# Order of the dense units as a list, half weight tiles, banks for each half of the first chunk, and the last adds on GpSimd

## The chip, the core and the metric

The kernel runs on one core of one Trainium2 chip. Its engines are TensorE (PE; PEld is its weight load), VectorE (DVE), ScalarE (ACT), GpSimd (POOL) and SyncE (SP, which here only issues transfers). Each engine executes its own instructions in the order in which they stand in the program and waits for the others by semaphores. The metric is the device time of one execution in microseconds (us); less is better. The time before is 863.67 us, the median of 3 runs (863.49 to 864.08).

## What is computed

The input is 2048 tokens of 512 features. A layer norm feeds two branches: windowed attention with 32 heads of 16 features, in which each token sees itself and the 255 before it, and a SwiGLU feed-forward with 1792 hidden features. The second branch gates the first.

```python
xn = layernorm(x)                                  # 2048 x 512
q, k, v = split_heads(xn @ wqkv)                   # 32 heads of 16
scores = where(0 <= i - j < 256, q @ k.T * 16**-0.5, -1e9)
s = (softmax(scores) @ v) @ wo
f = (silu(xn @ w_gate) * (xn @ w_up)) @ w_down
out = x + s * silu(f)
```

All is fp32. Each operand of a dense matmul is split in a high part (the value rounded to the type fp32r) and a low part (what is left), and three products, high with high, high with low and low with high, are added up.

## The kernel before

The kernel is a program that writes out a schedule. While it is built, it keeps a clock of its own for each engine, and hands out instructions in the order in which that clock says they can run; the chip then runs this fixed order.

The 2048 tokens are four chunks of 512. The dense work is cut in 120 units, each with one weight tile of up to 128 x 1024 values. `Proj` (A) makes q and k of two groups of four heads, `Values` (V) makes v of half the heads, `GateUp` (G) makes one block of 128 hidden features, `Down` (D) adds a quarter of the hidden features to half of the output columns, `Wo` (W) is the attention's output product for half of the columns. A name like G1.7 is chunk 1, block 7. `dense_order` sets the order of the units from due times of A and V and a fixed row of G, D and W. A unit has two items, one bank of PSUM each, and PE's array is used as two halves of 64 rows: each half does its 64 features of an item, then the halves change items. A small DVE copy (`handover`, tile `ho`) stands between the two.

Between the dense matmuls PE runs the attention of 32 groups of heads: `b` are scores for the row maximum (DVE adds the mask and takes the maximum, tile `jk`), `c` are scores again, of which ACT makes the exponentials `p` and POOL masks the edges, and `pv` is the product with v. q and k go through DRAM (`qkd`) to be laid out anew, and so do the outputs of the attention (`od`, and the sums' reciprocals `den`, `rd`, read back as `o` and `r`).

For each unit, SP fetches its weights into a raw tile (`wr`, by `w_fetch`), ACT copies the high part (`wh`, L413) and POOL subtracts to get the low part (`wl`, L418), in pieces of 512 columns. There are three pairs of tiles of 1024 columns, so unit j can be split when unit j - 3 has ended (`w_split`, `item_end`), and unit j + 2 is fetched when unit j is split.

At the start (the head), the four token tiles of chunk 0 are loaded, normalised on ACT or DVE (`xt`, with the root `rs` made on POOL), and turned on PE into four banks `xp`, one for each 128 features, with all 512 tokens in one bank (`x_turn`). ACT then copies the high part `xh` (L332) and DVE subtracts the low part `xl` (L320), for tokens 0 to 255 and 256 to 511 apart. Dense matmuls begin when all four tiles are turned. The first unit is A0.0. Until then PE runs matmuls on a tile of ones (`warm`).

At the end (the tail), W3.0 and W3.1 are the last units, the last with four items of 128 tokens. `finish` multiplies an item by the gate (L813), adds x (L820) and stores it; in the last chunk all of this is on DVE, in the others the sum is on POOL.

Of the kernel before, what the change touches and what calls it, by code (L numbers as in the profile page):

```python
# [10 lines left out]
F32R = mybir.dt.float32r  # L11
# [6 lines left out]
P = 128  # L18
# [22 lines left out]
SPARE = 3  # L41
MW = 80
# [12 lines left out]
def tile_window_attention_swiglu_gate(  # L55
# [138 lines left out]
    def constants2():  # L194
# [117 lines left out]
    turned = []  # L312

    def x_split(k, part, pb, t, free):
        n = slice(256 * part, 256 * part + 256)
        hi, lo = (xn[0][s][:, k, n] for s in range(2))

        def low(t):
            xhigh[k, part] = t
            do("V", t, 0.42, lambda: nc.vector.tensor_tensor(lo, pb[:, n], f32(hi), op=ALU.subtract), done, -0.5)  # L320

        def done(t):
            xlow[k, part] = t
            if part == 0:
                return
            free(t)
            xready[0, k] = t
            if k == KC - 1:
                for i in range(4):
                    give(xt.pop((0, i)))  # L330

        do("S", t, 0.33, lambda: nc.scalar.activation(hi, pb[:, n], AF.Copy), low, -2.0)  # L332
# [3 lines left out]
    def x_turn(i):  # L336
        if not turned:
            turned.extend((bank(p, f"xp0_{k}"), p) for k, p in enumerate((rb_free, rb_free, fb_free, fb_free)))
        for k in range(KC):
            nc.tensor.matmul(  # L340
                turned[k][0][0][:, i * P : (i + 1) * P], xt[0, i][:, k * P : (k + 1) * P], ident,
                is_transpose=True, start=True, stop=True,
            )
        advance(0.45)
        seen.add(i)
        part = i // 2
        if {2 * part, 2 * part + 1} <= seen:
            for k in range(KC):
                (pb, tag), p = turned[k]
# [11 lines left out]
    class Unit:  # L361
# [3 lines left out]
        def wts(self, r):  # L365
            return wtile[self.n]


# [6 lines left out]
    ended_unit = {}  # L375

    def w_fetch(j):
# [16 lines left out]
        dma(now[0], go, then, slack=1.0, kb=512 if j > 2 else 400)  # L394

    raw = {}
    wpart = {}

    def w_split(j):
        if j not in landed or (j >= 3 and j - 3 not in ended_unit):  # L400
            return
        t = max(landed.pop(j), ended_unit.get(j - 3, 0.0))
        w = weighted[j].width
        hi, lo = [], []
        cuts = [(a, min(a + 512, w)) for a in range(0, w, 512)]
        left = [len(cuts)]

        def high(a, b):
            if not hi:
                hi.append(sb(f"wh{j}", [P, 1024], F32R, "wh", 3))  # L410
                lo.append(sb(f"wl{j}", [P, 1024], F32R, "wl", 3))
                wtile[j] = [hi[0], lo[0]]
            nc.scalar.activation(hi[0][:, a:b], raw[j][:, a:b], AF.Copy)  # L413

        def low(a, b):
            if j == 0 and a == 0:
                nc.gpsimd.tensor_copy(spare, xt[0, list(normed)[-1][1]][:, :1])
            nc.gpsimd.tensor_tensor(lo[0][:, a:b], raw[j][:, a:b], f32(hi[0][:, a:b]), op=ALU.subtract)  # L418

        def done(t, a):  # L420
            wpart[j, a, 1] = t
            left[0] -= 1
            if left[0] == 0:
                wready[j] = t
                if j:
                    timer(t - 0.5, w_fetch, j + 2)

        def after_high(t, a, b, sl):
            wpart[j, a, 0] = t
            do("G", t, 0.17 + 0.0021 * (b - a), lambda: low(a, b), lambda t: done(t, a), sl, lambda: len(normed) >= 4)  # L430

        for n, (a, b) in enumerate(cuts):
            sl = (0.0 if j >= 3 else 0.2) + 0.3 * n
            if j == 0:
                sl = -3.0 + 0.1 * n
            do("S", t, 0.13 + 0.00078 * (b - a), lambda a=a, b=b: high(a, b),
               lambda t, a=a, b=b, sl=sl: after_high(t, a, b, sl), sl)
# [3 lines left out]
    def item_end(j, t):  # L441
        item_ended[j] = item_ended.get(j, 0) + 1
        if item_ended[j] == 2 * weighted[j].items:
            ended_unit[j] = t
            w_split(j + 3)
# [8 lines left out]

    def xt_ready(c, k):
        return latest([*(normed.get((c, t)) for t in range(4)), bank_time(rb_free, 2)])
# [36 lines left out]
    PAIRS = ((0, 0), (0, 1), (1, 0))  # L493

    class Stationary(Unit):
# [3 lines left out]

# [7 lines left out]
        def mms(self, i, r, pb):  # L507
            w = [t.rearrange("p (a k n) -> p a k n", a=2, k=KC) for t in self.wts(r)]
            xs = xn[self.c % 2]
            if self.c == 0 and self.n == 0 and i == r:  # L510
                for a, b in ((0, 0), (1, 0), (0, 1)):
                    for part in range(2):
                        n = slice(256 * part, 256 * part + 256)
                        for k in range(KC):
                            def go(first, last, k=k, a=a, b=b, n=n):
                                return mm(pb[:, n], w[a][half(r), i, k, :], xs[b][half(r), k, n], first, last)
                            yield 256, go, lambda k=k, a=a, b=b, part=part: latest(
                                [(xlow if b else xhigh).get((k, part)), wpart.get((0, 512 * i, a))]
                            )
# [958 lines left out]
```

## Time and profile before

| what | value |
| --- | --- |
| median of 3 runs | 863.67 us |
| the profiled execution, its time | 865.33 us |
| its span, first to last instruction | 863.6 us |
| granted TensorE clock, mean | 0.998 |
| PE busy | 854.2 us (99%), 11960 matmuls |
| PEld, POOL, ACT, DVE busy | 785.1, 595.9, 495.7, 486.2 us |
| DMA | 139.58 MB, mean 162 GB/s |

The profile is of one execution. A row of a timeline gives the start and the length in us, the engine, the line, the work with its tiles as out<-in, and how many instructions it covers; in brackets stands the idle time of the engine just ahead of it and what ended that. A row of PE's waits gives who was waited for, then the total in us, how many waits, and the longest. The chain of waits follows the last instruction back to what released it. Tiles' numbers are left out in these rows.

### The profile page before, as it was taken

To read this page: it belongs to the slowest core of one execution; us is meant where nothing else is said; L and a number is where in the kernel's file an instruction comes from. 1 tells how busy PE (TensorE), PEld (TensorE's weight loads), DVE (VectorE), ACT (ScalarE), POOL (GpSimd) and SP (SyncE) were. 2 spreads that over 40 slices of the span, in tenths; PEclk is the share of its full clock that TensorE was granted. 3 is DMA by queue.
4 is the path that set the end of the run, shared out by engine and by line. 5 is a ranking of instruction groups with operands and counts; after the bars stand their busy time and mean duration, and the time that the engine had idled before them with its cause. 6 is when DMAs were issued, how large, how long until landed. Compare 5 with 4: busy or idle time off the path is not lost.

```text
span 863.6 us, 29615 instructions
## 1 busy us (share of the span) xinstructions
PE 854.2 (99%) x11960; PEld 785.1 (91%) x11960; DVE 486.2 (56%) x1633; ACT 495.7 (57%) x1056; POOL 595.9 (69%) x630
## 2 busy tenths in 40 slices
PE   9999999999999999999999999999999999999997
PEld 8999999899799898999799999999999989889897
DVE  4364566555566555656565656566556656645234
ACT  4355555546665566565677566655656665656532
POOL 7555566658776775666879586666668697869764
PEclk9999999999999999999999999999999999999999
DMA  5764645455756963464777866455556668553241
GB/s 176 198 179 132 195 112 172 142 156 153 195 154 183 275 171 111 96 181 123 174 201 185 223 183 192 108 174 136 165 135 174 176 188 223 166 147 113 87 149 62
DMA packets 67628, 139.58 MB, mean 162 GB/s; under 512 B 12690, under 2 KB 21394, under 8 KB 67492
## 3 DMA queue, kind: packets, MB, share of 16 engines
q1 hardware_dynamic: 67204, 137.17, 57.3%
q8 instruction: 94, 1.54, 0.8%
q10 hardware_dynamic: 288, 0.52, 0.2%
q14 instruction: 42, 0.34, 0.2%
HBM read 107.74 MB, written 29.62 MB: 159 GB/s over the span
## 4 chain that ended last, share of the span: by engine, by line
PE 94%; DMA 3%; DVE 1%; ACT 1%; issue 0%; SPq 0%; POOL 0%; DVEq 0%; POOLq 0%; ACTq 0%
PE u L451 18%; PE d L451 18%; PE g L451 18%; PE a L451 11%; PE pv L1152 8%; PE c L1115 5%; PE s L451 5%; PE vp L451 5%; PE b L961 5%; DMA r<-rd 1%; DMA wr<-wgu 1%; DVE jk L969 0%; DMA xt<-x 0%; PE xp L469 0%; ACT wh L413 0%
## 5 line engine op out<-in xcount | busy, mean ns | idle before, releaser
L418 POOL TENSOR_TENSOR wl<-wr,wh 128x512 fp32r<-128x512 f32 x240 | 296.7, 1259 | 166.0 <-ACT wh L413 146.9
L969 DVE CUSTOM_DVE_ANT_0 jk<-b,maskb 128x384 bf16<-128x384 f32 (+2 forms) x512 | 271.7, 531 | 152.1 <-PE b L961 87.4
L1076 ACT ACTIVATE p<-c 128x384 f32<-128x384 f32 (+1 forms) x480 | 206.8, 496 | 87.1 <-PE c L1115 78.5
L451 PE MATMUL d<-wh,hh 64*128 64x256 f32 x1792 | 236.7, 278 | 0.0
L451 PEld LDWEIGHTS d<-wh,hh 64*128 64x128 f32 x1792 | 208.7, 185 | 1.4 <-issue 0.8
L451 PE MATMUL d<-wl,hh 64*128 64x256 f32 x896 | 191.7, 279 | 0.0
L413 ACT ACTIVATE wh<-wr 128x512 fp32r<-128x512 f32 x240 | 136.4, 616 | 69.1 <-issue 15.6
L451 PE MATMUL g<-xh,wh 64*128 64x512 f32 x448 | 173.3, 395 | 0.0
L451 PE MATMUL g<-xl,wh 64*128 64x512 f32 x448 | 172.9, 395 | 0.0
L451 PE MATMUL g<-xh,wl 64*128 64x512 f32 x448 | 172.6, 394 | 0.0
L451 PE MATMUL u<-xh,wh 64*128 64x512 f32 x448 | 172.2, 395 | 0.0
L451 PE MATMUL u<-xl,wh 64*128 64x512 f32 x448 | 171.6, 395 | 0.0
L451 PE MATMUL u<-xh,wl 64*128 64x512 f32 x448 | 171.4, 395 | 0.0
L451 PEld LDWEIGHTS d<-wl,hh 64*128 64x128 f32 x896 | 143.1, 185 | 0.4
L961 PE MATMUL b<-k,q 48*128 48x384 f32 (+1 forms) x512 | 113.3, 339 | 2.0 <-ACT p L1076 2.0
L1089 POOL TENSOR_SCALAR_AFFINE_SELECT p<-p 128x512 f32<-128x512 f32 x128 | 81.1, 637 | 48.9 <-ACT p L1076 44.3
L1115 PE MATMUL c<-q,k 49*128 49x384 f32 (+1 forms) x704 | 106.2, 305 | 0.7 <-ACT p L1076 0.7
L451 PE MATMUL a<-xh,wh 64*128 64x512 f32 (+1 forms) x264 | 88.6, 396 | 0.2 <-DVE ho L448 0.2
L451 PE MATMUL a<-xl,wh 64*128 64x512 f32 (+1 forms) x264 | 87.5, 387 | 0.0
L451 PE MATMUL a<-xh,wl 64*128 64x512 f32 (+1 forms) x264 | 86.8, 386 | 0.0
L451 PEld LDWEIGHTS g<-xh,wl 64*128 64x128 f32 x448 | 82.3, 186 | 3.0
L451 PEld LDWEIGHTS g<-xl,wh 64*128 64x128 f32 x448 | 82.0, 185 | 3.1 <-issue 0.2
(102 smaller groups left out, 2039.6 us busy)
## 6 DMA issues: line engine op xcount, KB each, us to landing
wr<-wgu SPq DMA_DIRECT2D x56, 512.0 KB
k<-qkd SPq DMA_DIRECT2D x48, 192.0 KB
wr<-wqk SPq DMA_DIRECT2D x16, 512.0 KB
qkd<-qkh SPq DMA_DIRECT2D x32, 256.0 KB
qkd<-qkl SPq DMA_DIRECT2D x32, 256.0 KB
q<-qkd SPq DMA_DIRECT2D x64, 128.0 KB
wr<-wdn SPq DMA_DIRECT2D x16, 512.0 KB
od<-ev SPq DMA_DIRECT2D x32, 256.0 KB
```

The lines of the kernel that those rows point to most:

```text
L413: nc.scalar.activation(hi[0][:, a:b], raw[j][:, a:b], AF.Copy)
L418: nc.gpsimd.tensor_tensor(lo[0][:, a:b], raw[j][:, a:b], f32(hi[0][:, a:b]), op=ALU.subtract)
L451: return nc.tensor.matmul(pb, a, b, start=first, stop=last, skip_group_check=True)
L961: nc.tensor.matmul(pb[:, :w], qs[u % 3][r : r + 48, p, qb * P : (qb + 1) * P], ks[u % 3][r : r + 48, p, lo : lo + w], start=True, stop=True,)
L969: nc.vector.tensor_tensor_reduce(junk[:, :n], pb[:, :n], maskb[:, 3 * P - n :], 1.0, -3.0e38, ALU.add, ALU.max, m[:, col : col + 1],)
L1076: nc.scalar.activation(t[:, h, :], pc[:, a:b], AF.Exp, scale=DH ** -0.5)
L1089: nc.gpsimd.affine_select(s, s, [[0, 4], [1, P]], ALU.is_ge, 0.0, base=0, channel_multiplier=-1)
L1115: nc.tensor.matmul(pc[:, at0 : at0 + w], ks[u % 3][r : r + 49, p, k0 : k0 + P], qs[u % 3][r : r + 49, p, qb * P : qb * P + w], start=(i == ...
L1152: nc.tensor.matmul(pbs[r][0][32 * j : 32 * j + 32, q0:q1], vt[half(r), (4 * c + kb) % VT, VW * (4 * g + j) : VW * (4 * g + j) + 32], t[hal ...
```

## The change

**The order.** `ORDER` lists the same 120 units one by one, and takes the place of what `dense_order` gave. Its beginning, and that of before:

```text
before: A0.0 G0.0 G0.1 G0.2 A0.1 G0.3 G0.4 V0.0 G0.5 D0.0.0 A0.2 D0.0.1 V0.1 G0.6 ...
after:  A0.0 G0.0 A0.1 G0.1 G0.2 A0.2 G0.3 G0.4 G0.5 V0.0 D0.0.0 G0.6 G0.7 D0.0.1 ...
```

Units 23 to 35 in either order (in the fetches of weights below, `wr30` is the unit at place 30 from 0):

```text
before: A1.0 D0.2.0 D0.2.1 G0.13 G1.0 A1.1 D0.3.0 D0.3.1 G1.1 G1.2 G1.3 V1.0 A1.2
after:  G0.13 V0.1 A1.0 A1.1 D0.2.1 G1.0 D0.3.0 A1.2 G1.1 G1.2 D0.3.1 V1.0 G1.3
```

The two halves of a D often stand apart now, V comes later in its chunk, and two or three A stand close together. A new gate (`xleft`) holds the transposes of a chunk until all A and V of the chunk two before have ended.

**The weights.** The tiles are six pairs of 512 columns in place of three pairs of 1024. Half a of unit j is split when the half tile six halves earlier has been read for the last time, and an item of A or G waits for its own half alone. Work and pieces are as before, but for one: the high part of the second half of unit 0 is copied on POOL.

**The head.** Tokens 0 to 255 and 256 to 511 are turned into two banks each, with two blocks of features side by side in a bank. Dense matmuls may begin before all four tiles are turned. The first two items have an order of products of their own (`FIRST`). A memset of 15 columns of `v` is new on POOL.

**The tail.** In the last chunk the sums of `finish` are on POOL, but for the last item, which stays on DVE.

```diff
+        nc.gpsimd.memset(vt[:, :, H // 2 * VW : H // 2 * VW + 32 - VW], 0.0)
...
 def x_turn(i):
-        if not turned:
-            turned.extend((bank(p, f"xp0_{k}"), p) for k, p in enumerate((rb_free, rb_free, fb_free, fb_free)))
+        part = i // 2
+        if part not in turned:
+            turned[part] = [(bank(p, f"xp0_{part}_{n}"), p) for n, p in ((0, (rb_free, fb_free)[part]), (1, (rb_free, fb_free)[part]))]
...
+    def w_cut(j, a):
+        old = divmod(2 * j + a - NW, 2)
+        if j not in landed or (j, a) in wtile or (old[0] >= 0 and old not in wfreed):
             return
...
+        if (j, a) == (0, 1):
+            do("G", t, 0.6, lambda: nc.gpsimd.tensor_copy(hi, raw[j][:, n]), after_high, sl)
+        else:
+            do("S", t, 0.13 + 0.00078 * m, lambda: nc.scalar.activation(hi, raw[j][:, n], AF.Copy), after_high, sl)
...
+    def item_end(n, t):
+        j, i = n
+        u = weighted[j]
+        item_ended[n] = item_ended.get(n, 0) + 1
+        for a in range(2):
+            if (j, a) not in wfreed and all(item_ended.get((j, i)) == 2 for i in u.uses(a)):
+                wfreed[j, a] = t
+                w_cut(*divmod(2 * j + a + NW, 2))
...
     def xt_ready(c, k):
+        if xleft.get(c - 2):
+            return None
...
+    FIRST = (
+        ((0, 0, 0), (1, 0, 0), (0, 1, 0), (0, 0, 1), (1, 0, 1), (0, 1, 1)),
+        ((0, 0, 0), (0, 1, 0), (0, 0, 1), (1, 0, 0), (1, 0, 1), (0, 1, 1)),
+    )
...
-            (nc.vector if last else nc.gpsimd).tensor_tensor(box["y"], box["y"], t, op=ALU.add)
+            (nc.vector if e == "V" else nc.gpsimd).tensor_tensor(box["y"], box["y"], t, op=ALU.add)
...
-            do("V" if last else "G", t, 0.61 if last else 1.24, add, after_add, 2.0,
+            e = "V" if last and per == 1 and i == 3 else "G"
+            do(e, t, {"V": 0.35, "G": 0.65}[e] if per == 1 else 1.24, lambda: add(e), after_add, 2.0,
...
-    order = dense_order()
+    order = planned(ORDER) if ORDER else dense_order()
...
-        if heads or xstart[0]:
-            return None
```

Three places show what moved. The first is POOL at the head; `rs` is the root of a token tile, `wr0` the raw weights of unit 0, `xt0_2` the last token tile to come. Before:

```order
L256 TENSOR_TENSOR rs0_91<-ve0_90,power_84 128x1
L258 TENSOR_SCALAR tm0_92<-mv0_89,rs0_91 128x1
L256 TENSOR_TENSOR rs0_91<-ve0_90,power_84 128x1 x2
L417 COPY spare_93<-xt0_2_126 128x1
L418 TENSOR_TENSOR wl0_194<-wr0_132,wh0_193 128x512 x2
```

The same place afterwards:

```order
L269 TENSOR_SCALAR tm0_92<-mv0_89,rs0_91 128x1
L267 TENSOR_TENSOR rs0_91<-ve0_90,power_84 128x1
L451 CAST wh0_1_137<-wr0_133 128x512
L267 TENSOR_TENSOR rs0_91<-ve0_90,power_84 128x1
L437 COPY spare_93<-xt0_2_127 128x1
L438 TENSOR_TENSOR wl0_0_136<-wr0_133,wh0_0_135 128x512
```

The copy of the second weight half now stands between the roots of the third and of the fourth token tile.

The second is PE at the head afterwards, from the transposes of the third token tile to come (`xt0_3`) on; before, all sixteen transposes stand ahead of the first `a`:

```order
L353 MATMUL xp0_1_0_208<-ident_68,xt0_3_125 128x128 x2
L353 MATMUL xp0_1_1_209<-ident_68,xt0_3_125 128x128 x2
L246 MATMUL warm_87<-warm_85 128x128 x2
L470 MATMUL a0_0_222<-xh0_79,wh0_0_135 128x256
L470 MATMUL a0_1_224<-xh0_79,wh0_1_137 128x256
L470 MATMUL a0_0_222<-xh0_79,wh0_0_135 128x256
L470 MATMUL a0_1_224<-xh0_79,wh0_1_137 128x256
L246 MATMUL warm_87<-warm_85 128x128
L353 MATMUL xp0_1_0_208<-ident_68,xt0_2_127 128x128 x2
L353 MATMUL xp0_1_1_209<-ident_68,xt0_2_127 128x128 x2
```

Four of the 48 matmuls of the first two items stand ahead of the last token tile's transposes, the rest behind.

The third is SP around the fetches of weight units 31 to 33, for whose weights ACT and then PE wait (`qkd` from `qkh`, `qkl` are stores of q and k, `q` and `k` their loads for attention). Before:

```order
L94 DMA wr31_3888<-wgu 128x1024
L94 DMA rd_67<-den0_2_3703 128x32
L94 DMA qkd_65<-qkh1_2_3934 8x16x512
L94 DMA q1_73<-ms7_3955 2x8x128
L94 DMA qkd_65<-qkl1_2_3935 8x16x512
L94 DMA qkd_65<-qkh1_3_3973 8x16x512
L94 DMA od_66<-ev6_3961 128x512
L94 DMA qkd_65<-qkl1_3_3974 8x16x512
L94 DMA wr32_4050<-wgu 128x1024
L94 DMA wr33_4113<-wgu 128x1024
L94 DMA q0_72<-qkd_65 32x2x512
L94 DMA q0_72<-qkd_65 16x2x512
```

Afterwards, from the last of the eight q and k loads between fetches 30 and 31 (ahead of which stand an od store and three qkd stores behind fetch 30) to the loads behind fetch 32:

```order
L104 DMA k2_77<-qkd_65 16x2x768
L104 DMA qkd_65<-qkh1_3_3779 8x16x512
L104 DMA wr31_3907<-wgu 128x1024
L104 DMA qkd_65<-qkl1_3_3780 8x16x512
L104 DMA den0_2_3935<-od_66 128x1x32
L104 DMA o0_0_3948<-od_66 128x1x512
L104 DMA o0_1_3958<-od_66 128x1x512
L104 DMA wr32_3972<-wgu 128x1024
L104 DMA r0_0_3949<-rd_67 128x1x512
L104 DMA r0_1_3959<-rd_67 128x1x512
```

Fetches 32 and 33 no longer stand side by side, and the stores and loads that stood around them are now mostly ahead of fetch 31.

More of the change, by code (lines that the diff above doesn't have):

```diff
@@ L392, in then @@
             w_split(j)
-        dma(now[0], go, then, slack=1.0, kb=512 if j > 2 else 400)
+        dma(now[0], go, then, slack=1.0, kb=512 if j > 2 else 400 if j else 200)
     raw = {}
     wpart = {}
+    wfreed = {}
+    NW = 6
     def w_split(j):
-        if j not in landed or (j >= 3 and j - 3 not in ended_unit):
-            return
[L402 to L415, printed above, removed]
+        for a in range(2):
+            w_cut(j, a)
+    def w_cut(j, a):
+        old = divmod(2 * j + a - NW, 2)
+        if j not in landed or (j, a) in wtile or (old[0] >= 0 and old not in wfreed):
+            return
+        n = slice(512 * a, min(512 * a + 512, weighted[j].width))
+        m = n.stop - n.start
+        wtile[j, a] = [
+            pers.tile([P, 512], F32R, name=f"w{s}{j}_{a}", tag=f"w{s}{(2 * j + a) % NW}", bufs=1) for s in "hl"
+        ]
+        hi, lo = (t[:, :m] for t in wtile[j, a])
+        sl = (0.0 if j >= 3 else 0.2) + 0.3 * a
+        if j == 0:
+            sl = -3.0 + 0.5 * a
+        def low():
@@ L432, in w_split @@
[L432 to L437, printed above, removed]
-    item_ended = {}
[L441 to L445, printed above, removed]
+            nc.gpsimd.tensor_tensor(lo, raw[j][:, n], f32(hi), op=ALU.subtract)
@@ L649, in go @@
                                 pb[:, t * 256 : t * 256 + 256], self.act(k, a)[half(r), tok],
-                                w[b][half(r), k, :], first, last,
+                                w[k // 2][b][half(r), k % 2, :], first, last,
                             )
@@ L1277, in dense_order, with planned @@
         return order
-    order = dense_order()
+    def planned(names):
+        kinds = {"A": Proj, "V": Values, "G": GateUp, "D": Down, "W": Wo}
+        return [kinds[n[0]](*map(int, n[1:].split("."))) for n in names.split()]
+    order = planned(ORDER) if ORDER else dense_order()
+    for u in order:
+        if isinstance(u, (Stationary, Values)):
+            xleft[u.c] = xleft.get(u.c, 0) + 2 * u.items
     weighted = {}
@@ L1401, in tile_window_attention_swiglu_gate @@
             continue
-        if xstart[0] and now[0] >= 4.1:
+        times = [ready(0), ready(1)]
+        able = [r for r in range(2) if times[r] is not None and times[r] <= max(clock[r], now[0])]
+        if xstart[0] and not able and now[0] >= 4.1:
             warm_up(warm, 1)
@@ L1405, in tile_window_attention_swiglu_gate @@
             continue
-        times = [ready(0), ready(1)]
-        able = [r for r in range(2) if times[r] is not None and times[r] <= max(clock[r], now[0])]
         done = False
```

93 lines of the change are left out of this document (51 added, 42 removed), and 8 rows, old and new, of the table ORDER.

## Prediction

> **What bounds the kernel now.** I read the page first, then the waits of PE, the chain of waits, and the timelines of the first 16 us, of the one bad place in the middle, and of the last 5 us.
>
> ```profile
> span 863.6 us, 29615 instructions
> PE 854.2 (99%) x11960; PEld 785.1 (91%) x11960; DVE 486.2 (56%) x1633; ACT 495.7 (57%) x1056; POOL 595.9 (69%) x630
> PE 94%; DMA 3%; DVE 1%; ACT 1%; issue 0%; SPq 0%; POOL 0%; DVEq 0%; POOLq 0%; ACTq 0%
> ```
>
> PE is busy for 854.2 of 863.6 us and carries 94% of the chain. The change neither adds nor removes a matmul of the dense units, so it can only win in the 9.4 us in which PE is idle, or by how the same matmuls stand beside each other. Where the idle time lies, PE's own waits tell:
>
> ```profile
> PE b L961 <- ACT p L1076: 2.0, 2, 1.3
> PE c L1115 <- ACT p L1076: 0.7, 1, 0.7
> ```
>
> The two b waits and the c wait (2.7 us) are all that the middle shows. The rest, 6.7 us, is the head, and the tail, in which PE has no work.
>
> **The head.** These rows are the timelines of POOL, ACT, DVE and PE (start, length, work; in brackets the idle time ahead and what ended it).
>
> ```profile
> 7.81 0.55 POOL L256 TENSOR_TENSOR rs<-ve,power 128x1 f32<-128x1 f32 x1
> 8.81 0.78 POOL L256 TENSOR_TENSOR rs<-ve,power 128x1 f32<-128x1 f32 x1 [0.45 <-DVE ve L251]
> 10.24 0.18 POOL L417 COPY spare<-xt 128x1 f32<-128x1 f32 x1 [0.65 <-DVE xt L274]
> 10.38 2.53 POOL L418 TENSOR_TENSOR wl<-wr,wh 128x512 fp32r<-128x512 f32 x2
> 8.49 1.14 ACT L413 ACTIVATE wh<-wr 128x512 fp32r<-128x512 f32 x2
> 10.82 2.04 ACT L332 ACTIVATE xh<-xp 128x256 fp32r<-128x256 f32 x7 [0.83 <-PE xp L340]
> 9.63 0.55 DVE L274 TENSOR_SCALAR xt<-xt,mv,rs 128x512 f32<-128x512 f32 x1 [0.44 <-POOL rs L256]
> 10.40 0.60 PE L340 MATMUL xp<-ident,xt 128*128 128x128 f32 x4
> 13.14 1.07 PE L451 MATMUL a<-xh,wl 64*128 64x256 f32 x16
> 14.05 1.07 PE L451 MATMUL a<-xl,wh 64*128 64x256 f32 x16
> 15.37 0.57 PE L451 MATMUL a<-xh,wh 64*128 64x512 f32 x2 [0.24 <-DVE ho L448]
> ```
>
> Before, seven of the eight xh copies wait until 10.82, for transposes that write the same banks, and PE's first 16 matmuls run at the copies' pace; the next 16 take from 13.14 to 14.05, which is 0.057 us each.
>
> Afterwards: with banks of their own for tokens 0 to 255, the four xh copies of that part need only the second tile's transposes and can follow ACT's first wh copy, whose second is gone from ACT: from about 9.25, four at 0.28, done by 10.4. What I expect to set the pace instead is POOL. Its new copy of the second weight half stands between the two rs rows above, so between 8.36 and the last rs, and that rs releases the last xt, its transposes, and through the small copy both wl. No row has a 128x512 copy with one input on POOL. Its bounds are these two groups:
>
> ```profile
> L196 POOL MEMSET one<- 128x512 f32 x1 | 0.5, 525 | 0.0
> L1089 POOL TENSOR_SCALAR_AFFINE_SELECT p<-p 128x512 f32<-128x512 f32 x128 | 81.1, 637 | 48.9 <-ACT p L1076 44.3
> L418 POOL TENSOR_TENSOR wl<-wr,wh 128x512 fp32r<-128x512 f32 x224 | 285.6, 1296 | 166.0 <-ACT wh L413 146.9 <-PE g L451 5.8 <-PE b L961 4.9
> L418 POOL TENSOR_TENSOR wl<-wr,wh 128x256 fp32r<-128x256 f32 x16 | 11.8, 740 | 0.0
> 5.87 0.58 POOL L256 TENSOR_TENSOR rs<-ve,power 128x1 f32<-128x1 f32 x1 [1.68 <-DVE ve L251]
> ```
>
> The memset has no input (0.53), the sum of two inputs takes 1.30; the affine select, one input and one output, is the nearest, 0.64. The copy then runs 8.36 to 9.0, the last rs starts at 9.0 in place of 8.81, and everything behind it is 0.2 us late: xt at 10.4, transposes done at 11.2, the first wl at 11.85 (10.38 + 1.27 + 0.2), the second at 13.1. Eight of the 48 first matmuls are done by then; the other 40 follow the first wl: 11.95 + 40 x 0.057 = 14.25, plus 0.2 for the last to drain, 14.45, against 15.12 before (14.05 + 1.07). The second wl is wanted by the 22nd of them, at 13.15, just in time. **Head: 0.65 us less.** With the copy at 0.53 it is 0.8; at 1.30 the chain is 0.85 late and the gain is 0. The new memset of v (about 0.25) stands ahead of the 1.68 us that POOL idles before its first rs, and costs nothing unless that idle time goes.
>
> **The tail.** The end of DVE's and SP's timelines and of the chain:
>
> ```profile
> 858.55 0.42 DVE L813 SCALAR_TENSOR_TENSOR y<-gp,s 128x256 f32<-128x256 f32 x1 [0.41 <-PE s L451]
> 859.13 0.42 DVE L813 SCALAR_TENSOR_TENSOR y<-gp,s 128x256 f32<-128x256 f32 x1 [0.16 <-PE s L451]
> 859.47 1.09 DVE L820 TENSOR_TENSOR y<-y,xr 128x256 f32<-128x256 f32 x3
> 859.91 1.31 SPq L94 DMA_DIRECT2D out<-y  x3
> 854.94 4.09 PE s L451 x61
> ```
>
> PE ends at 859.03. Three adds then run one after the other on DVE, and three stores leave SP 0.45 us apart, the last about 860.8. Afterwards DVE has only the fourth item's add, right behind its product: 859.5 to 859.9. The items before it are added on POOL: the third's product is there at 858.97, its add takes 0.74 (the 128x256 group above), to 859.8, its store goes at about 859.85, and the fourth's at 860.3. **Tail: 0.5 us less.** Were SP's spacing not there it would be 0.9; were the POOL add as long as the 1.30 of a full tile, the two stores would leave at 860.4 and 860.85: 0. The earlier items have microseconds to spare.
>
> **The middle.** The order of the 120 units changes from about the third on, and the halves of a weight tile come free apart. That moves which transfers meet. The bad place of before, in SP's timeline, the chain and the windows (in a window's row, PE's busy time comes first, and the DMA share and GB/s last):
>
> ```profile
> 215.74 2.66 SPq L94 DMA_DIRECT2D wr<-wgu  x2
> ...
> 215.74 10.22 DMA wr<-wgu
> 225.98 1.15 ACT wh L413 x2
> 227.13 0.39 ACT p L1076
> 227.56 0.44 PE b L961
> ...
> 220.00:225.00 5.00, 5.00 (x66) 4.98 (x64) 1.88 (x10) 3.67 (x9) 3.20 (x6) 1.00 0.95 220
> 225.00:230.00 5.00, 3.26 (x33) 2.37 (x29) 2.88 (x8) 3.26 (x7) 3.75 (x4) 1.00 0.57 143
> ```
>
> Two weight fetches go out back to back behind four qkd stores and an od store, and the first takes 10.22 us. ACT works in order: the weight's copy waits for it, the exponentials (p) stand behind that copy, and PE's b wait for banks that p frees: 2.0 us in two waits. In the order afterwards this knot is undone: the pair is split and the four stores go out earlier. I take the 2.0 as gone, leave the 0.7 of the c wait, and give back 0.3 for a new wait of the size of the small rows above. **Middle: 1.7 us less**, between 2.7 less (all waits gone) and, if the knot only comes back elsewhere, nothing. How the halves of the array pair up in another order I put at 0; it could be 2 us either way, a quarter of a percent of PE's time (an estimate, no row prices it). The gate on the transposes of later chunks costs nothing: the units that it waits for stand more than ten units earlier in the list.
>
> **Sum.** 0.65 + 0.5 + 1.7 = 2.85 us. The span goes from 863.6 to 860.75; the profiled execution took 865.33, 1.73 more than its span, and would be 862.5. The median of the runs is 863.67, 1.66 under that execution, so 860.8.
>
> **Rivals.** *The waits only move.* Head and tail gain 1.15, the middle nothing: 862.5. For it speaks that the fetches and the q and k loads are as many as before, so some must still meet; against it that before shows one such knot in 120 units.
>
> *A worse knot, slower.* The sizes:
>
> ```profile
> DMA packets 1632, 3.41 MB, mean 155 GB/s; under 512 B 341, under 2 KB 357, under 8 KB 1626
> wr<-wgu SPq DMA_DIRECT2D x2, 512.0 KB
> qkd<-qkl SPq DMA_DIRECT2D x2, 256.0 KB
> k<-qkd SPq DMA_DIRECT2D x2, 192.0 KB
> q<-qkd SPq DMA_DIRECT2D x2, 128.0 KB
> k<-qkd SPq DMA_DIRECT2D x2, 96.0 KB
> q<-qkd SPq DMA_DIRECT2D x2, 64.0 KB
> ```
>
> (one answer, for 208 to 230 us). The new order has three projections of the next chunk close together (A1.0, A1.1, A1.2), so that between the fetches of weight units 30 and 32 SP issues an od store and five qkd stores (256 KB each), the eight q and k loads (960), fetch 31 (512) and two o loads (512): 3.5 MB, where before 1.8 MB stood from the stores up to and with fetch 32. At the 155 GB/s of these rows that is 23 us, against two units of 7.2 us (863.6 / 120): the fetch lands some 9 us late. If PE loses 6 of them, the sum is 863.7 - 1.15 - 2.0 + 6.0 = 866.5. It decides from 4.9 us of waits on, where the change comes out 0.2% slower. Against it: at the 220 GB/s of the full window above, the same bytes take 16 us and the fetch is hardly late. The Trainium skill, page "DMA: Bandwidth & Descriptors", section "Queues, rings and completion order", has all transfers that one engine issues on one row of rings, whose descriptors are consumed in ring order, so that a fetch pays for the bytes ahead of it and not for those behind. By that rule the place to fear is the one with the most bytes ahead, this one; the trace agrees with it so far (1.8 MB at 155 to 220 GB/s are 8 to 12 us, and the fetch took 10.22).
>
> *The head does not gain*, since the copy on POOL takes 1.30 us: 861.5.
>
> **Chances.** The forecast 0.50, the waits only move 0.27, the worse knot 0.15, no gain at the head 0.08. A measurement of this kernel tells 0.2% (1.7 us) from no change. Faster: 0.50 + 0.08 = 0.58; same 0.27; slower 0.15. Low end: 863.7 less 0.8, 0.9, 2.7 and the 2 of the pairing, 857.3; the high end, 865, leaves out most of the worse knot.
>
> **What would show it.** Head right: the four first xh end before 10.5 and the first 512-wide a starts near 14.7, not 15.4; wrong if POOL's copy is over 1 us. Tail right: the last store leaves 1.3 us behind PE's end, not 1.8. Middle right: PE's waits on ACT's p at or under 1 us together; wrong if one wr of 10 us or more stands in the chain with ACT's wh behind it, between 195 and 225 us above all. I would be wrong altogether if PE's busy time itself moved by microseconds.

## The result, and the profile after

The changed kernel takes 858.23 us, the median of 4 runs (857.99 to 858.46), against 863.88 us for the kernel before, run beside it: a ratio of 0.9931, with a 95% interval from 0.9916 to 0.9946. That is 5.65 us less, where 2.85 were forecast. The sign and the range were right; the size was half. The head and the tail came out nearly as worked out. The middle gave about three times its 1.7 us (2.6 times by the medians, 3.3 times in the profiled executions), and most of that from a place that the prediction had put at 0.

The page of the changed kernel, its chain of waits by engine, and its only wait in the middle:

```profile
span 856.7 us, 29715 instructions
PE 848.9 (99%) x11960; PEld 785.9 (92%) x11960; DVE 486.0 (57%) x1628; ACT 497.9 (58%) x1055; POOL 602.7 (70%) x637
PE 95%; DMA 3%; DVE 1%; ACT 0%; issue 0%; POOL 0%; SPq 0%; DVEq 0%; ACTq 0%; POOLq 0%
PE c L1146 <- ACT p L1107: 2.0, 2, 1.0
```

Before, PE was busy for 854.2 us. It now executes as many matmuls in 5.3 us less, at the same granted clock (a mean of 0.998 before, 0.999 after). PE's waits in the middle went from 2.7 us (b 2.0, c 0.7) to 2.0.

**The head.** The rows that answer to those of before, from the timelines of POOL, ACT and PE:

```profile
8.35 0.61 POOL L451 CAST wh<-wr 128x512 fp32r<-128x512 f32 x1
8.93 0.72 POOL L267 TENSOR_TENSOR rs<-ve,power 128x1 f32<-128x1 f32 x1
10.45 2.52 POOL L438 TENSOR_TENSOR wl<-wr,wh 128x512 fp32r<-128x512 f32 x2
9.15 1.21 ACT L343 ACTIVATE xh<-xp 128x256 fp32r<-128x256 f32 x4
14.76 0.73 PE L470 MATMUL a<-xh,wh 64*128 64x512 f32 x2
```

The copy on POOL takes 0.61 us (0.64 was the estimate), the first four xh end at 10.36, and the first 512-wide a stands at 14.76 in place of 15.37: 0.61 us less, 0.65 forecast.

**The tail**, from the same views and SP's:

```profile
852.05 1.41 POOL L850 TENSOR_TENSOR y<-y,xr 128x256 f32<-128x256 f32 x2 [0.80 <-POOL y L850]
853.35 0.42 DVE L850 TENSOR_TENSOR y<-y,xr 128x256 f32<-128x256 f32 x1
849.34 4.95 SPq L104 DMA_DIRECT2D out<-y  x6
852.52 0.28 PE L470 MATMUL s<-wh,xl 64*128 64x256 f32 x1
```

PE ends at 852.80, and the span 3.9 us later; before, it was 863.6 - 859.03 = 4.57. That is 0.7 us less, 0.5 forecast. An add on POOL takes 0.71.

**The middle.** From the first 512-wide a to PE's end it was 843.66 us (859.03 - 15.37) and is 838.04 (852.80 - 14.76): 5.6 us less in the profiled executions. That of before ran 1.45 us above its runs' median and that of after 0.23 above its own, so by the medians the middle gave about 4.4. The knot around 216 to 230 us is gone, and the one that I feared at the fetches 30 to 32 did not come: between 195 and 230 us the chain of waits is on PE alone. These rows are the issues of fetches 31 and 32, ACT's copies of unit 32's weights, and a window from the issue of fetch 30 to that of fetch 32 (its last three numbers are the granted clock, the DMA share and GB/s):

```profile
204.48 0.36 SPq L104 DMA_DIRECT2D wr<-wgu  x1
208.16 0.45 SPq L104 DMA_DIRECT2D wr<-wgu  x1
217.97 1.15 ACT L453 ACTIVATE wh<-wr 128x512 fp32r<-128x512 f32 x2 [1.22 <-PE d L470]
190.80:208.16 17.36, 17.36 (x219) 17.00 (x217) 10.62 (x42) 8.77 (x20) 7.55 (x9) 1.00 0.80 218
```

Fetch 31 landed 6.0 us after its issue. Fetch 32, ahead of which the prediction had counted 3.5 MB, had landed by 217.97, at most 9.8 us after its issue, and its copies had waited for PE to release their tiles, not for the fetch. In the 17.36 us before its issue 3.8 MB moved (218 GB/s), so most of the bytes counted ahead of it were already through.

Two smaller ones stand elsewhere. One of them, from the chain:

```profile
55.98 7.58 DMA wr<-wdn
...
64.18 0.61 ACT wh L453
64.79 0.39 ACT p L1107
...
65.22 0.77 PE c L1146 x5
```

It is the knot of before in small: a late weight, its copy on ACT, the exponentials behind that copy, and PE's next scores. The other, at 466 us, begins with a load of o that takes 10.97 us, behind which POOL, ACT's `oh` and the exponentials wait in turn.

### The profile page after: what moved, and what is told of

Same layout as the page of the kernel before. It is cut to its first block, busy times and chain, and to the rows that moved or that the text cites. A ratio compares the mean times of both kernels' runs of the same rounds, so it can differ in the third digit from the quotient of the medians.

```text
span 856.7 us, 29715 instructions
## 1 busy us (share of the span) xinstructions
PE 848.9 (99%) x11960; PEld 785.9 (92%) x11960; DVE 486.0 (57%) x1628; ACT 497.9 (58%) x1055; POOL 602.7 (70%) x637
## 4 chain that ended last, share of the span: by engine, by line
PE 95%; DMA 3%; DVE 1%; ACT 0%; issue 0%; POOL 0%; SPq 0%; DVEq 0%; ACTq 0%; POOLq 0%
PE g L470 18%; PE d L470 18%; PE u L470 18%; PE a L470 11%; PE pv L1183 8%; PE c L1146 6%; PE s L470 5%; PE b L992 5%; PE vp L470 4%; DMA o<-od 1%; DMA wr<-wdn 1%; DMA xt<-x 0%; PE xp L492 0%; DVE jk L1000 0%; PE xp L353 0%
## 5 line engine op out<-in xcount | busy, mean ns | idle before, releaser
L470 PE MATMUL d<-wh,hh 64*128 64x256 f32 x1792 | 254.3, 279 | 0.0
L470 PEld LDWEIGHTS d<-wh,hh 64*128 64x128 f32 x1792 | 219.8, 186 | 0.6 <-issue 0.2
L470 PE MATMUL d<-wl,hh 64*128 64x256 f32 x896 | 197.6, 279 | 0.0
L453 ACT ACTIVATE wh<-wr 128x512 fp32r<-128x512 f32 (+1 forms) x239 | 143.1, 620 | 91.8 <-PE u L470 22.7
L470 PE MATMUL u<-xl,wh 64*128 64x512 f32 x448 | 169.8, 394 | 0.0
L470 PE MATMUL u<-xh,wh 64*128 64x512 f32 x448 | 169.3, 395 | 0.0
L992 PE MATMUL b<-k,q 48*128 48x384 f32 (+1 forms) x512 | 109.6, 335 | 0.0
L1146 PEld LDWEIGHTS c<-q,k 49*128 49x128 f32 x704 | 79.8, 186 | 6.5 <-ACT p L1107 2.7
L470 PEld LDWEIGHTS g<-xh,wh 64*128 64x128 f32 x448 | 81.9, 186 | 2.7 <-DVE ho L467 0.4
L470 PEld LDWEIGHTS u<-xl,wh 64*128 64x128 f32 x448 | 81.2, 186 | 2.8 <-issue 0.4
```

The lines of the kernel that those rows point to most:

```text
L453: do("S", t, 0.13 + 0.00078 * m, lambda: nc.scalar.activation(hi, raw[j][:, n], AF.Copy), after_high, sl)
L470: return nc.tensor.matmul(pb, a, b, start=first, stop=last, skip_group_check=True)
L992: nc.tensor.matmul(pb[:, :w], qs[u % 3][r : r + 48, p, qb * P : (qb + 1) * P], ks[u % 3][r : r + 48, p, lo : lo + w], start=True, stop=True,)
L1146: nc.tensor.matmul(pc[:, at0 : at0 + w], ks[u % 3][r : r + 49, p, k0 : k0 + P], qs[u % 3][r : r + 49, p, qb * P : qb * P + w], start=(i == ...
```

## The experiments

What the waits don't explain is 4 us of PE's busy time. Three theories stood against each other: the list of units alone brings it (L), the half tiles bring it (T), or it lies in how the matmuls of the array's two halves alternate in the finished program, which any rebuilding changes, so that the list is good only with the build that it was made for (J).

**How the idle halves are read.** Each dense matmul uses 64 of the 128 rows. Two on different halves overlap, two on one half follow each other; while one half has nothing to do, the page still shows PE as busy. From each run's trace I took the start of every matmul and the half that it works on, with 117 ns for 256 columns (the spacing on one half, shown below) and 223 for 512, and added up the gaps of a half over 0.13 us, from the end of the head on: apart the part in which the other half works, divided by two (what PE loses by it), and the part in which both stand still, which holds the waits. Where the clock is granted at half, as in three of the runs below, matmuls stand further apart, and the columns hold a part of that too.

| run | median us | ratio to before, 95% | span | PE busy | one half idle | both idle |
| --- | --- | --- | --- | --- | --- | --- |
| before | 863.9 to 864.4 | | 863.6 | 854.2 | 8.4 | 5.8 |
| the changed kernel | 858.23 | 0.9916 to 0.9946 | 856.7 | 848.9 | 3.8 | 4.6 |
| changed_again | 858.51 | 0.9920 to 0.9951 | 856.3 | 848.5 | 3.8 | 4.5 |
| old_order | 863.23 | 0.9974 to 0.9991 | 861.6 | 855.1 | 8.7 | 3.3 |
| list_alone | 871.97 | 1.0070 to 1.0100 | 869.6 | 858.7 | 11.5 | 8.7 |
| freed_together | 870.56 | 1.0043 to 1.0084 | 867.9 | 858.3 | 10.9 | 7.8 |
| before_nudged | 874.43 | 1.0091 to 1.0126 | 872.9 | 865.7 | 16.0 | 7.7 |
| after_nudged | 872.42 | 1.0087 to 1.0113 | 870.5 | 862.2 | 13.8 | 5.5 |
| searched_list | 859.82 | 0.9929 to 0.9962 | 859.1 | 851.7 | 4.2 | 7.6 |
| moved_list_cast | 857.28 | 0.9904 to 0.9929 | 855.6 | 848.6 | 3.0 | 3.8 |
| second_list_cast | 857.50 | 0.9911 to 0.9935 | 855.0 | 849.6 | 4.4 | 2.6 |

**old_order**: the list is left out, all else is as changed.

```diff
-    order = planned(ORDER) if ORDER else dense_order()
+    order = dense_order()
```

> The changed kernel with the list left out: the units stand in the order that dense_order gives, all else (half tiles, head, tail) is as changed. Theory L (the list alone brings the middle's gain): head and tail keep their 1.2 us, the middle's 5.6 us are gone, so about 862.5 with PE's waits on p near 2.7 us again. Theory T (the half tiles bring it): about 858.5, PE busy near 849. Theory J (list and build were fitted to each other; what the gain is made of is how the matmuls of the two halves of the array alternate in the finished program, and any other build of the same units alternates worse): slower than 862.5. A count along PE's program, in which each half takes its matmuls one after the other at the lengths of the rows, gives 5.3 us more idle halves than in the changed kernel, so about 863.6 by J, with PE busy near 854 and no more than 3 us of waits.

Measured: 863.23 us. Against the 864.44 beside it that is what head and tail give, and nothing for the middle. The page's line on the engines and PE's longest wait in the middle:

```profile
PE 855.1 (99%) x11960; PEld 789.3 (92%) x11960; DVE 484.0 (56%) x1628; ACT 495.7 (58%) x1055; POOL 602.4 (70%) x637
PE a L470 <- DVE ho L467: 0.3, 1, 0.3
```

The waits on p are gone without the list, 2.7 us to none, and one of 0.3 on a handover is left. PE's busy time is 6.2 us over the changed kernel's, and 0.9 over that of before. T is out as the only cause, and so is my account of the middle by waits: here is a program without the knot, and by the medians it is no faster for that.

**list_alone**: the kernel before with the list, and whole tiles.

```diff
+ORDER = (...)
...
+        if xleft.get(c - 2):
+            return None
...
-    order = dense_order()
+    order = planned(ORDER) if ORDER else dense_order()
```

> The kernel before with the list (and the gate on the transposes and the small memset that it needs), with whole weight tiles, the old head and the old tail. Theory L: the middle's 5.6 us come, head and tail do not, so about 858.3. Theory T: nothing comes, 863.7. Theory J: slower than before; the same count gives 5.8 us more idle halves than before, so about 869 by J, nearly all of it in PE's busy time.

Measured: 871.97 us. L is out. One wait in it is of a sort of its own:

```profile
PE 858.7 (99%) x11960; PEld 795.1 (91%) x11960; DVE 487.5 (56%) x1633; ACT 493.5 (57%) x1056; POOL 595.3 (68%) x631
PE c L1130 <- DMA q<-qkd: 3.9, 1, 3.9
```

In this build a load of q for group 8 comes ahead of the last scores of group 5, which wait for it and are made from it, so those scores are wrong; the amount of work is the same. The wait costs more than itself. Two windows of equal length, ahead of it and behind it (PE's busy time and its matmuls come first, the granted clock stands third from the end):

```profile
183.00:187.80 4.80, 4.80 (x100) 3.71 (x98) 1.29 (x5) 2.46 (x5) 2.52 (x2) 1.00 0.24 60
197.80:202.60 4.80, 4.80 (x34) 4.80 (x36) 2.20 (x10) 0.87 (x2) 1.22 (x2) 0.50 0.60 151
```

Behind the wait the granted clock is 0.50, and 512-wide matmuls on one half follow each other at 0.42 us (198.25 and 198.67, for one) in place of 0.23: some 2 us are lost in this window (an estimate from the two spacings). Without the wait and this loss it would be about 866, still 1 to 2 us slower than before, where L had 858.3.

**freed_together**: the changed kernel, in which an item waits for both halves of its weight tile, and they come free together.

```diff
         def uses(self, a):
-            return (a,)
+            return range(self.items)
         def need(self, i):
-            return wpart.get((0, i)) if self.n == 0 else wready.get((self.n, i))
+            return wpart.get((0, i)) if self.n == 0 else latest(wready.get((self.n, a)) for a in range(2))
```

> The changed kernel in which both halves of a weight tile are waited for and come free together, as whole tiles did; list, head and tail as changed. Theory L: 858.3, as changed. Theory T: the middle's gain is gone, about 863. Theory J: the count gives 8.6 us more idle halves than in the changed kernel, so about 866 to 867, slower than before, though nothing but the freeing of the tiles is undone.

Measured: 870.56 us, 12 more than the changed kernel and more than J's count. PE's waits and busy time:

```profile
PE 858.3 (99%) x11960; PEld 797.7 (92%) x11960; DVE 486.6 (56%) x1628; ACT 496.7 (57%) x1055; POOL 602.2 (69%) x637
PE c L1146 <- ACT p L1107: 1.7, 2, 1.4
PE b L992 <- ACT p L1107: 1.1, 1, 1.1
```

The list with tiles freed together is slower than no list at all: 10.9 us of one idle half against 8.7.

**before_nudged** and **after_nudged**: nothing of the change is touched; a constant of the schedule moves a little.

```diff
-PACE = 17.6
+PACE = 17.58
```

> The kernel before with PACE = 17.58 in place of 17.6: the same units, tiles, head and tail, only due times in the schedule that move by a thousandth. Theories L and T: nothing that they speak of is touched, 863.7 within 0.5. Theory J: the finished program alternates otherwise; the count gives 7.3 us more idle halves than before, so about 870 by J, in PE's busy time.

Measured: 874.43 us, 10 us more than before.

```diff
-STEP = 0.05
+STEP = 0.06
```

> The changed kernel with STEP = 0.06 in place of 0.05, the step by which the schedule's clock moves on where nothing can be issued. List, half tiles, head and tail are as changed. Theories L and T: 858.2. Theory J: the matmuls of the halves stand otherwise; the count gives 11.5 us more idle halves than in the changed kernel, so about 870, with PE busy near 860: the whole gain is lost to a change of a number that is in no part of the change.

Measured: 872.42 us, 14 us more than the changed kernel. Both lose it in PE's busy time:

```profile
PE 865.7 (99%) x11960; PEld 805.9 (92%) x11960; DVE 485.0 (56%) x1633; ACT 494.2 (57%) x1056; POOL 595.6 (68%) x630
```

```profile
PE 862.2 (99%) x11960; PEld 800.9 (92%) x11960; DVE 484.9 (56%) x1628; ACT 496.7 (57%) x1055; POOL 602.3 (69%) x637
```

In before_nudged a part of it is the clock, which is granted at half from 272.0 to 278.8 us, behind a stretch with many idle halves and short waits. Two windows, in it and behind it, both with matmuls of 256 columns:

```profile
274.10:278.70 4.60, 4.60 (x46) 4.60 (x46) 0.57 (x3) 0.87 (x2) 1.40 (x3) 0.50 0.96 306
279.10:281.70 2.60, 2.60 (x49) 2.60 (x48) 0.27 (x2) 0.00 (x0) 0.00 (x0) 1.00 0.74 182
```

That is some 3 of its 10 us (an estimate from the two counts, over 6.8 us). In after_nudged and freed_together the clock of the profiled execution is full to PE's end (a mean of 0.999), and there this has no part in the loss.

What the loss of a half looks like can be seen near the end of before_nudged, where only W3.1 is left. PE's timeline (start, length, count) and two windows (PE's busy time and its matmuls, then PEld's):

```profile
865.59 0.39 PE L451 MATMUL s<-wl,xh 64*128 64x256 f32 x2
865.71 0.38 PE L451 MATMUL s<-wh,xl 64*128 64x256 f32 x2
865.83 0.28 PE L451 MATMUL s<-wh,xh 64*128 64x256 f32 x1
865.95 0.28 PE L451 MATMUL s<-wl,xh 64*128 64x256 f32 x1
...
865.90:868.70 2.80, 2.80 (x28) 2.80 (x25) 1.93 (x6) 0.00 (x0) 0.00 (x0) 1.00 0.56 189
860.00:862.80 2.80, 2.80 (x52) 2.80 (x50) 1.54 (x5) 0.00 (x0) 1.32 (x2) 1.00 0.00 0
```

Up to 865.71 two matmuls come every 0.12 us, one for each half. From 865.83 on it is one every 0.117: the other half has run out of items. In the first window PE is busy for 2.80 of 2.80 us with 28 matmuls, in the second for just as long with 52 of the same kind. No wait, no gap and no share of the page tells them apart; the count does. The kernel before had such a place too, in the unit D0.3.0, just ahead of the knot:

```profile
212.60:214.20 1.60, 1.60 (x19) 1.60 (x16) 0.93 (x3) 1.60 (x4) 1.35 (x2) 1.00 0.42 65
```

16 matmuls on one half follow each other there while the other half is idle for 1.65 us, the longest such gap of before; in the changed kernel the longest is 0.8. The Trainium skill, page "TensorEngine Tiling (Array Packing)", section "Key Properties", says that the tiles of a divided array work independently and in parallel; the trace agrees, with 0.117 us from matmul to matmul on one half and half of that on two. The Trainium skill's page "Perfetto Trace Analysis", section "Identifying the Most-Contended Engine", warns that matmul busy time is a bad measure of how much is left to gain, and the two windows at 866 and 860 us bear it out. It advises two others, the arithmetic done per time (MFU) and the busy share of weight loads. The second is no better here: 2.80 of 2.80 us in both.

**tail_on_dve**: all sums of the last chunk on DVE, PE's order unchanged.

```diff
-            e = "V" if last and per == 1 and i == 3 else "G"
+            e = "V" if last else "G"
```

> The changed kernel with all sums of the last chunk on DVE again; PE's instructions stand in the same order as in the changed kernel. By the prediction's tail step: 0.5 us more, 858.7, and the last store leaves SP 1.8 us behind PE's end in place of 1.3. If the tail's gain came from elsewhere: 858.2, no change.

Measured: 858.61 us, 0.9923 to 0.9949, which the interval does not part from the changed kernel. Its rows do:

```profile
853.34 0.27 PE L470 MATMUL s<-wh,xl 64*128 64x256 f32 x1
854.11 0.76 DVE L850 TENSOR_TENSOR y<-y,xr 128x256 f32<-128x256 f32 x2
850.20 5.17 SPq L104 DMA_DIRECT2D out<-y  x6
```

The last store is through SP 1.76 us behind PE's end (855.37 - 853.61); in the changed kernel it is 1.49 (854.29 - 852.80), and before it was 2.19 (861.22 - 859.03). So of the tail's 0.7 us, POOL brings some 0.3; the other 0.4 is there with all sums on DVE, whose products and sums now take turns, where before three sums stood behind the last product.

**cast_on_act**: the copy of the second weight half of unit 0 is on ACT again.

```diff
-        if (j, a) == (0, 1):
+        if False:
```

> The changed kernel with the high part of the second weight half of unit 0 copied on ACT, as before. By the prediction's head step POOL sets the pace there: the last rs starts at about 8.8 in place of 8.93, everything behind it is 0.1 us earlier, the first 512-wide a near 14.65, time 858.1. The rival: ACT sets the pace, the four xh copies wait 0.6 us behind the second wh, the first 512-wide a is near 15.2 and the time 858.7. PE's order behind the head is nearly unchanged (the count of idle halves is 0.1 us less).

Measured: 857.00 us, 0.9908 to 0.9932. The head's rows:

```profile
8.66 1.13 ACT L453 ACTIVATE wh<-wr 128x512 fp32r<-128x512 f32 x2
9.70 1.18 ACT L343 ACTIVATE xh<-xp 128x256 fp32r<-128x256 f32 x4
8.97 0.78 POOL L267 TENSOR_TENSOR rs<-ve,power 128x1 f32<-128x1 f32 x1 [0.45 <-DVE ve L262]
14.79 0.77 PE L470 MATMUL a<-xh,wh 64*128 64x512 f32 x2
```

All of this execution's head is 0.13 us later than the changed kernel's (its first xt on ACT starts at 7.02 against 6.89). Less that, the first 512-wide a stands at 14.66, and 14.65 was expected: POOL sets the pace, as the prediction had it, and the xh, 0.4 us later by the same measure, hold nobody up. Moving the copy to POOL costs 0.1 us and gains nothing. The median is 1.2 us under the changed kernel's 858.23, of which the head's rows explain 0.1; the intervals of the two overlap, and the rest is not explained.

**old_banks**: old_order with the four banks of the first chunk as before; one execution.

```diff
-            turned[part] = [(bank(p, f"xp0_{part}_{n}"), p) for n, p in ((0, (rb_free, fb_free)[part]), (1, (rb_free, fb_free)[part]))]
+            turned.extend((bank(p, f"xp0_{k}"), p) for k, p in enumerate((rb_free, rb_free, fb_free, fb_free)))
```

> The kernel of the run old_order with the four banks of the first chunk laid out as before (one for each 128 features, all 512 tokens in a bank); only the first 16 us are read. If the banks bring the head's gain: the first four xh no longer end together near 10.45, all but one wait for the last transposes, and the first 512-wide a is at 15.4 in place of 14.84. If the gain comes from POOL's copy or the order of the first products: it stays within 0.15 of 14.84.

```profile
9.62 0.94 ACT L343 ACTIVATE xh<-xp 128x256 fp32r<-128x256 f32 x3 [0.53 <-PE xp L351]
11.56 1.49 ACT L343 ACTIVATE xh<-xp 128x256 fp32r<-128x256 f32 x5 [1.01 <-PE xp L351]
8.88 0.72 POOL L267 TENSOR_TENSOR rs<-ve,power 128x1 f32<-128x1 f32 x1
15.04 0.70 PE L469 MATMUL a<-xh,wh 64*128 64x512 f32 x2
```

Neither expectation. From the start of the last rs to the first 512-wide a it was 6.56 us before (15.37 - 8.81), it is 5.83 in the changed kernel (14.76 - 8.93), 5.82 in cast_on_act and 6.16 here. The banks bring 0.33 of the head's 0.73 by this measure. The other 0.40 comes with what is left, most likely the order of the first products and the earlier start of the dense matmuls. Those two were not tried apart, and old_banks is one execution.

**searched_list**: another list, found by moving units and keeping what lowered a count of idle halves along PE's program. It puts D3.2.1 last, behind W3.1, so the right half of the last chunk goes out without that unit's part, and the program ends without the last products behind it.

```diff
-    ... D3.2.0 D3.2.1 D3.3.0 D3.3.1 W3.0 W3.1
+    ... D3.3.1 W3.0 W3.1 D3.2.1
```

> The changed kernel with another list: units moved by one to four places one after the other, kept where the count of idle halves along PE's program and the end of the schedule's own clock fell together. Theory J: the count is 3.1 us less than in the changed kernel, so about 855.1, by PE's busy time. The rival, that waits on transfers rule the middle: the list was not chosen for them, so as many knots come as go, 858 within 3, and PE busy near 849.

Measured: 859.82 us, no gain over the changed kernel.

```profile
PE 851.7 (99%) x11960; PEld 783.9 (91%) x11960; DVE 483.7 (56%) x1628; ACT 498.7 (58%) x1055; POOL 602.4 (70%) x637
PE c L1146 <- ACT p L1107: 3.2, 3, 1.5
```

The count promised 3.1 us; the trace shows 4.2 us of one idle half, no better than the 3.8 of the changed kernel, and 3 us more with both idle. The rival was nearer: the list was chosen without its waits, and they came. Here too the clock is granted at half behind one of them, from 470.1 to 473.5 us. The three executions that read a mean clock of 0.998 took 860.8 to 861.6 us, the three at 0.999 and 1.0 took 856.9 to 858.8, so what the list does without this is about what the changed kernel does.

**changed_again, moved_list_cast, second_list_cast**: the changed kernel as a control, and two more lists, both with the copy of unit 0 on ACT. A list's first line:

```diff
-    "A0.0 G0.0 A0.1 G0.1 G0.2 A0.2 G0.3 G0.4 G0.5 V0.0 D0.0.0 G0.6 G0.7 D0.0.1 G0.8 G0.9 A0.3 G0.10 "
+    "A0.0 G0.0 A0.1 G0.1 G0.2 A0.2 G0.3 G0.4 G0.5 D0.0.0 V0.0 G0.6 G0.7 D0.0.1 G0.8 G0.9 A0.3 G0.10 "
```

> The changed kernel itself, beside the next two on one chip, as the control for them: 858.2 within 0.5, PE busy 848.9.

> The changed kernel with 40 units of the list moved by one to three places (every D of a column half in the order of its quarters, every W behind its D), chosen by the count of idle halves, and the copy of unit 0's second weight half on ACT. By the count as it stands: 3.4 us less than the changed kernel, 854.8. By what the searched list showed (a quarter of the count came, and the waits grew by 3 us): 0.9 us less from the halves and 0.1 from the copy, 857.2, if no wait is added; 860 if waits come as there.

> As the run before, with another such list (66 units moved, up to twelve places), found from another start. By the count: 3.1 us less than the changed kernel, 855.1; by what the searched list showed: 857.3 without added waits, 860 with them. If the two lists differ by more than a microsecond though their counts are 0.3 apart, the count alone doesn't choose between lists, and waits on transfers do.

Measured: 858.51, 857.28 and 857.50 us. The pages of the two lists, each with its wait in the middle:

```profile
PE 848.6 (99%) x11958; PEld 784.7 (92%) x11958; DVE 485.2 (57%) x1628; ACT 497.5 (58%) x1056; POOL 603.1 (70%) x636
PE c L1146 <- ACT p L1107: 1.6, 2, 1.0
```

```profile
PE 849.6 (99%) x11958; PEld 782.3 (91%) x11958; DVE 484.1 (57%) x1628; ACT 497.9 (58%) x1056; POOL 602.7 (70%) x636
PE c L1146 <- ACT p L1107: 0.2, 1, 0.2
```

Both are about 1 us under the control, as the smaller of their two expectations said (857.2 and 857.3), and both come at it differently: the first by fewer idle halves (3.0 against 3.8), the second by fewer waits. The intervals (0.9904 to 0.9929, 0.9911 to 0.9935) overlap with the control's (0.9920 to 0.9951), so that they beat the kernel before is measured, and that they beat the changed one is likely, no more. Nor can the lists be credited with it: cast_on_act, with the list of the changed kernel and the same copy on ACT, took 857.00, a ratio of 0.9920 to the kernel before, against 0.9916 and 0.9923 here.

**What follows.** J holds: the time goes where halves have nothing to do, and a small rebuilding is enough to lose it. With both columns of idle time taken off the span, 847.3 to 851.2 us are left in every row, while the spans lie up to 17.9 us apart. In the table the spans go with the idle halves and the idle pairs together: from before to before_nudged they grow by 9.5 us, and the span by 9.3; from the changed kernel to freed_together by 10.3 and the span by 11.2; to old_order by 3.6, and the span by 4.9. In before_nudged a part of this is the half clock; in freed_together and after_nudged none is. From before to the changed kernel they fall by 5.8, of which 4.6 is one half idle and 1.2 both. Why a half has nothing to do at a given place (no free bank, a weight not yet split, an item not handed over) was tried for the weights alone: in freed_together that one condition costs 7.1 us of one idle half. Which of these conditions the changed program meets less often than the one before stays open.

## Why the prediction was right, and where not

**Head**, 0.65 forecast, 0.61 measured. The copy's price (0.64 for 0.61) and the pace set by POOL held. That the copy is itself a loss of 0.1 us, I had in the sum (the last rs 0.2 us late) without saying that leaving it on ACT would be better.

**Tail**, 0.5 forecast, 0.7 measured. The POOL add took 0.71 us as worked out (0.74). The last store behind PE's end I had at 1.8 and 1.3, by its issue; through SP it was 2.19 and 1.49.

**Middle, the waits.** "I take the 2.0 as gone": both b waits went. "Give back 0.3 for a new wait" was too little: c waits went from 0.7 to 2.0, so 0.7 us net by the waits' rows (1.2 by the idle pairs), not 1.7. The changed kernel run again shows a c wait of 1.7. My own sign for the middle, waits on p at or under 1 us together, failed with 2.0, though the wr of 10 us that I named as its cause is not there: the longest wr in the chain takes 7.58, and the load of 10.97 is one of o.

**Middle, the halves.** The step that failed is "How the halves of the array pair up in another order I put at 0; it could be 2 us either way". It was 4.6 us, more than all the terms of the sum together, and outside the bounds that I gave it. I had named the pairing beside the waits and then taken PE's 99% as a floor that only waits could lower, though the rows that show half of PE idle stood in the same trace, at 212.6 us, ahead of the very knot that I quoted. The line "I would be wrong altogether if PE's busy time itself moved by microseconds" came true: it moved by 5.3. The two errors of the middle, 1.0 us too much from the waits and 4.6 too little from the halves, add up to 3.6 of the 3.9 us by which it beat the forecast in the profiled executions. That the time still fell into the range is luck as far as the middle goes: it did so because its low end held all waits gone and 2 us of pairing, and because by the medians the middle gave 4.4 us and not 5.6.

**The rivals.** "The waits only move" was half true: they did move, and the gain came elsewhere. The worse knot at the fetches 30 to 32 did not come: fetch 32 took at most 9.8 us, where the bytes counted ahead of it would have taken 16 to 23. The step that failed there is the count: it took the bytes issued ahead of the fetch for bytes still to be moved, and 3.8 MB had moved in the 17.4 us in which they were issued. The rule on rings in the Trainium skill's page "DMA: Bandwidth & Descriptors", section "Queues, rings and completion order", is neither borne out nor contradicted by that. "The head does not gain" was wrong by its condition, since the copy took 0.61.

## What to carry to other kernels

A TensorE that works as two halves can be busy all the time and lose half of its rate: count the matmuls of one kind in windows of equal length, or look for rows of one in place of rows of two, before calling its busy time a floor. Where a planner writes the program, run a nudge of one of its constants before crediting an edit: here a thousandth of one due-time constant cost 10 us (some 7 without the half clock) and a hundredth of a microsecond in a clock step 14, each more than the whole change. A hand-written order is then a part of the build that it was found with; list and half tiles gain 4 us together, while the list alone loses 1 to 2 beside a wait of its own and the half tiles alone gain nothing, so they can be judged only together. Look at the granted clock of each run before a loss is put down to anything else: here a stretch at half clock cost up to 3 us of what an edit seemed to cost.

## What the runs showed of the hardware

GpSimd's copy of 128x512 from fp32 to fp32r takes 0.61 us, less than half of its subtraction of two such tiles (1.26 to 1.30). On one half of the array 256 columns take 0.117 us from start to start, and the other half fills in between, so that two halves together reach 0.06. In the window with one half the weight loads read as busy all the time too, with half as many of them (25 for 50), so that neither of PE's two busy rows shows an idle half.

In and behind stretches in which PE stood idle or half idle, the granted clock was 0.50 for 6.8 us in list_alone (at a wait of 3.9 us) and in before_nudged, and for 3.4 us in searched_list (after a wait of 1.5). A 512-wide matmul on one half then came every 0.42 us in place of 0.23. The changed kernel run again has a wait of 1.7 us without it, so no run here shows what sets it off.
